# Attention scores in blocks of 57 queries by 64 keys, two to a tile, with the value product in quadrants of the array

## The chip, the core and the metric

The kernel runs on one core of a Trainium2 chip. The metric is the device time in microseconds (us), the median of several runs; smaller is better. The engines are TensorE (PE; its weight loads are PEld), VectorE (DVE), ScalarE (ACT), GpSimd (POOL) and SyncE (SP), the last two used here mostly to issue transfers (DMA). TensorE writes to PSUM, which here is one tensor `PS` of four slots with two banks each.

## What is computed

Everything is bfloat16, S = 2048 rows, D = 640. `x = A_q`, and the result is `g * a + (1 - g) * b` with `g = sigmoid((x * gate_w).sum(-1))`.

- `a` is a long convolution: `k` goes through a four-tap causal filter, is multiplied by `v`, convolved over the whole length with the kernels `ssm_k` (an FFT of length 4096 in the reference), and multiplied by `x`.
- `b` is local attention with 32 heads of 20 channels. A query looks at 8 keys, 2 apart, itself included:

```python
qkv = (x @ wqkv).reshape(B, S, 3, H, Dh)          # H = 32, Dh = 20
idx = pos[:, None] - off[None, :]                 # off = 0, 2, 4, ..., 14; only idx >= 0 counts
logits = einsum("bhsd,bhswd->bhsw", q, kg) * Dh ** -0.5
o = einsum("bhsw,bhswd->bhsd", softmax(logits), vg)
b = o.reshape(B, S, D) @ wo
```

## The kernel before

Even and odd rows are kept apart (`xT`: 1024 rows of each parity), so that the 8 keys of a query become 8 neighbours. Attention then works on blocks: 114 queries against 121 keys (114 + 7), 9 blocks for each parity, 18 in all. Heads go in 8 sets `t` of four; each head of a set has its own 32 partitions in the key tile `kb` and the query tile `qb` (20 rows of data, 11 rows of a mask that makes every pair outside the band very negative). In the order of the data:

- `xpose` (L444) transposes x. `qkproj` (L573) makes q and k, 300 matmuls; its fragments go by DMA into `kb` and `qb` (`fragger`, L623, on POOL's and SP's queues). `vproj` (L526) makes `VW`, the v of one block with its keys on the partitions, and a column of ones behind each head's 20 channels.
- `score_gen` (L647): a group is 3 or 4 blocks by four heads. Each matmul has 31 contracted rows, 128 columns and 114 queries, with the four heads in the four row tiles of the array. Two exponentials (L658) turn a group into `ETall`, 121 x 912 or 121 x 684 elements. In the last two sets, filler matmuls (L652) into unused columns follow each group.
- `pv_gen` (L682): `ETall` is the stationary operand, 121 keys by 128 queries, `VW` the moving one. VectorE takes the reciprocal of the ones' column (L692) and multiplies (L694) into `oS`, which lies in `VW`'s memory.
- The convolution is done by transforms in two halves P = 0, 1: `s1_unit` (L709 for the data `u`, L713 for the kernel `h`), `s2_unit` (L732), `products` on VectorE (L764), `inverse1` (L843) and `final` (L930). `h_lin` holds one half of `ssm_k`; the second half is loaded when the first has been used (L324). `Hw` is a copy of `h` with its halves swapped by DMA (L828). `UC` takes the data's transform; its memory is that of the attention's tiles, so that it starts after the last value product.
- `op_tr` (L861) transposes `oS` into `oT`, one PSUM slot of bfloat16 for each of five `ft`, evicted by one copy of 2048 elements. `outproj` (L877) multiplies by `wo`; the evictions (L891) scale by 1 - g into `bl`, and `final` adds (L941, L943, L950) and stores (L952). The last tile goes another way (L882).
- `gate` (L539) makes g; its result takes four small transfers (L548) to come to its place.
- `copy` (L244 on ScalarE, L246 on VectorE) does most evictions, so its lines stand for many places; the tile names tell them apart.

What runs when is written out by hand in `ORDER`: a string with a letter for each stream (`a` is `xpose`, `d` is `score_gen`, `e` is `pv_gen`, and so on), where a letter lets that stream issue its next step and a `-` ahead of it picks VectorE in place of ScalarE (or the second of two engines). All engines work through their own queues in that order; PSUM slots are given out in it too (`take`, `give`). The costs in `Req` do not matter at run time.

Of the kernel before, what the change touches and what calls it, by code (L numbers as in the profile page):

```python
# [18 lines left out]
D = 640  # L19
# [8 lines left out]
BK = 121  # L28
NBP = 9
# [187 lines left out]
def kernel(  # L217
# [41 lines left out]
    ident = p0.tile([128, 128], BF, name="ident")  # L259
    F = p0.tile([128, 512], BF, name="F")  # L260
# [30 lines left out]
    ETall = pR.tile([128, NET, 2, 3 * BQ + 128], BF, name="ETall")  # L291
# [106 lines left out]
    def heads():  # L398
# [120 lines left out]
    def vproj(hp):  # L519
        for j in range(NBP):  # L520
            for par in range(2):
                g = yield Req("P", 0.0, xdeps(BQ * j - PRE, BQ * j - PRE + BK) + [ev(f"Wv{hp}")], take=1, half=1, pe=(5, 136.0, 272.0, 126.0))
                ps = psum(g)
                s0 = X0 + HP * par + BQ * j - PRE
                for dt in range(NDT):
                    nc.tensor.matmul(ps[0:BK, 0:320], lhsT=xT[:, dt, s0:s0 + BK], rhs=Wv[:, dt, 320 * hp:320 * hp + 320],  # L526
                                     start=(dt == 0), stop=(dt == NDT - 1))
# [465 lines left out]
```

## Time and profile before

| | |
|---|---|
| median of 3 runs | 220.84 us (220.32 to 221.04) |
| the profiled execution | 219.82 us, span 218.0 us, granted clock 0.99 |
| PE busy | 205.2 us (94% of the span), 3642 matmuls |
| DVE busy | 183.4 us (84%) |
| ACT busy | 173.5 us (80%) |
| exponentials (L658) | 63.9 us, 80 of them |
| q and k projection (L573) | 49.8 us, 300 matmuls |
| v projection (L526) | 27.5 us, 180 matmuls |
| value product (L682) | 18.5 us, 576 matmuls |
| scores (L647) | 15.6 us, 576 matmuls |

A group's row gives its line, engine, operation, what it writes and reads with the shapes, its count, then busy time in us and the mean ns of one, and the idle time ahead of it with what ended it. Matmuls overlap, so the mean ns of one says nothing of the pace: that is read from how long a run of them holds the chain. The chain of waits gives start, length and what ran.

### The profile page before, as it was taken

Reading aid. Unit: us, or ns where it says so; the run is one execution under the profiler, and the core shown is the slowest. Engines: PE = TensorE matmul, PEld = TensorE weight load, DVE = VectorE, ACT = ScalarE, POOL = GpSimd, SP = SyncE. Lnnn points to the kernel's source line nnn. Section 1 sums busy time; section 2 is a strip of 40 time slices with the busy share of each in tenths; the row PEclk is TensorE's granted clock in tenths of the full one; section 3 lists DMA queues with packets and bytes.
Section 4 is the critical chain, followed back from the end, with each engine's and each line's share of the span. In section 5 each row is a group of like instructions: output and inputs, shape, how many; then the busy total and the mean of one; then the engine's idle time right before and its main releaser. Section 6 shows DMA issues by size and latency. Waiting matters only on the chain.

```text
span 218.0 us, 8528 instructions
## 1 busy us (share of the span) xinstructions
PE 205.2 (94%) x3642; PEld 166.8 (76%) x3642; DVE 183.4 (84%) x264; ACT 173.5 (80%) x251; POOL 50.8 (23%) x129
## 2 busy tenths in 40 slices
PE   6999999999999999999997988999999999999990
PEld 3876987696677677656685766899888999998880
DVE  6647778997998998789897968998999997898782
ACT  0354387769998998989998988999899999487760
POOL 7980811460517045405420000000000000000000
PEclk9999999999999999999999699999999999999999
DMA  6999799699954993899984196767449064003544
GB/s 199 349 251 287 205 185 188 137 168 154 272 160 102 150 146 64 152 150 151 168 160 107 31 223 140 174 158 226 110 110 289 7 149 95 3 3 96 139 128 131
DMA packets 69049, 33.35 MB, mean 153 GB/s; under 512 B 51476, under 2 KB 66708, under 8 KB 69012
## 3 DMA queue, kind: packets, MB, share of 16 engines
q1 hardware_dynamic: 65684, 27.66, 62.0%
q0 software_dynamic: 2880, 4.90, 9.6%
q8 instruction: 28, 0.46, 1.0%
q10 hardware_dynamic: 448, 0.26, 0.4%
q14 instruction: 9, 0.07, 0.1%
HBM read 19.51 MB, written 2.62 MB: 102 GB/s over the span
## 4 chain that ended last, share of the span: by engine, by line
PE 66%; DVE 12%; ACT 6%; SPq 6%; DMA 5%; issue 3%; DVEq 0%; ACTq 0%
PE PS L573 16%; PE PS L526 12%; PE PS L877 10%; PE PS L843 8%; ACT ETall L658 5%; PE PS L682 5%; SPq L324 5%; PE PS L647 4%; PE PS L732 3%; DVE UC L246 3%; DMA h_lin<-in_A_ssm_k_dram 3%; DVE SX L246 3%; PE PS L930 2%; DMA WvT<-in_B_wqkv_dram 2%; PE PS L444 2%
## 5 line engine op out<-in xcount | busy, mean ns | idle before, releaser
L658 ACT ACTIVATE ETall<-PS 121x912 bf16<-121x912 f32 (+1 forms) x80 | 63.9, 865 | 6.4 <-PE PS L647 6.0
L573 PE MATMUL PS<-xT,Wqk 128*128 128x342 bf16 (+1 forms) x300 | 49.8, 310 | 0.7 <-ACT stg L244 0.3
L244 ACT CAST UC<-PS 128x1024 bf16<-128x1024 f32 (+2 forms) x49 | 44.4, 1030 | 4.0 <-DVE UC L246 3.1
L573 PEld LDWEIGHTS <-Wqk 128*128 128x128 bf16 x300 | 27.3, 97 | 14.6 <-issue 0.5
L526 PE MATMUL PS<-WvT,xT 128*121 128x320 bf16 x180 | 27.5, 301 | 0.6 <-DMA WvT<-in_B_wqkv_dram 0.3
L472 DVE TENSOR_TENSOR KX<-KX 128x1280 bf16<-128x1280 bf16 x32 | 25.3, 820 | 0.3
L526 PEld LDWEIGHTS <-xT 128*121 128x121 bf16 x180 | 23.5, 134 | 2.2 <-issue 0.4
L623 POOL DMA_DIRECT2D qb<-stg x29 | 14.5, 504 | 43.3 <-ACT stg L244 27.1
L877 PE MATMUL PS<-wo,oT 128*128 128x320 bf16 x160 | 24.5, 302 | 0.1
L244 ACT CAST stg<-PS 128x363 bf16<-128x363 f32 (+1 forms) x39 | 17.1, 472 | 8.5 <-PE PS L573 8.2
L877 PEld LDWEIGHTS <-oT 128*128 128x128 bf16 x160 | 21.0, 145 | 1.5 <-issue 0.5
L623 POOL DMA_DIRECT2D kb<-stg x36 | 18.0, 510 | 14.8 <-ACT stg L244 7.6
L732 PEld LDWEIGHTS <-G 64*128 64x128 bf16 x512 | 18.1, 93 | 3.8 <-issue 2.5
L682 PEld LDWEIGHTS <-ETall 121*128 121x128 bf16 x576 | 17.8, 97 | 1.6 <-issue 0.2
L682 PE MATMUL PS<-VW,ETall 121*128 121x63 bf16 (+2 forms) x576 | 18.5, 186 | 0.1
L843 PE MATMUL PS<-F,Hw 128*128 128x128 bf16 x160 | 18.1, 219 | 0.0
L843 PEld LDWEIGHTS <-Hw 128*128 128x128 bf16 x160 | 17.9, 114 | 0.0
L647 PE MATMUL PS<-qb,kb 31*128 31x114 bf16 x576 | 15.6, 212 | 2.3 <-ACT ETall L658 1.2
L246 DVE CAST UC<-PS 128x1024 bf16<-128x1024 f32 x13 | 15.3, 1220 | 2.6 <-ACT UC L244 1.2
L647 PEld LDWEIGHTS <-kb 31*128 31x128 bf16 x576 | 9.3, 93 | 10.3 <-issue 8.8
L246 DVE CAST SX<-PS 128x1024 bf16<-128x1024 f32 (+2 forms) x13 | 14.6, 1159 | 2.8 <-PE PS L732 1.7
L891 ACT ACTIVATE bl<-PS,omg 128x320 bf16<-128x320 f32 x30 | 15.4, 566 | 1.9 <-PE PS L877 1.4
(75 smaller groups left out, 329.9 us busy)
## 6 DMA issues: line engine op xcount, KB each, us to landing
xn<-in_A_q_dram SPq DMA_DIRECT2D x8, 320.0 KB
h_lin<-in_A_ssm_k_dram SPq DMA_DIRECT2D x16, 160.0 KB
vin<-in_A_v_dram SPq DMA_DIRECT2D x8, 320.0 KB
Hw<-H SPq DMA_DIRECT2D x8, 320.0 KB
q<-in_A_q_dram SPq DMA_DIRECT2D x8, 320.0 KB
Hw<-SX SPq DMA_DIRECT2D x8, 320.0 KB
kb<-stg POOLq DMA_DIRECT2D x28, 85.1 KB, 4.1
out_dram<-q SPq DMA_DIRECT2D x16, 120.0 KB
```

The costliest lines, as they stand in the source:

```text
L244: nc.scalar.copy(dst, src)
L246: nc.vector.tensor_copy(dst, src)
L472: eng.tensor_tensor(d, kin[:, n + 3 - j:n + 3 - j + m, :], w.to_broadcast([128, m, QC]), ALU.mult)
L526: nc.tensor.matmul(ps[0:BK, 0:320], lhsT=xT[:, dt, s0:s0 + BK], rhs=Wv[:, dt, 320 * hp:320 * hp + 320], start=(dt == 0), stop=(dt == NDT - 1))
L573: nc.tensor.matmul(ps[:, 0:n], lhsT=Wqk[:, dt, w, 128 * ft:128 * ft + 128], rhs=xT[:, dt, s0:s0 + n], start=(dt == 0), stop=(dt == NDT - 1))
L623: (nc.sync if near else nc.gpsimd).dma_start(dst[r0:r0 + rows, 0:wd], stg[fa - f0:fb - f0, 0:wd])
L647: nc.tensor.matmul(psum(g, h4 // 2)[:, h4 % 2, BQ * bb:BQ * bb + BQ], lhsT=kb[r:r + DH + NF, BK * b:BK * b + 128], rhs=qb[r:r + DH + NF, B ...
L658: nc.scalar.activation(ETall[0:BK, e, :, 0:BQ * nb], psum(g, k)[0:BK, :, 0:BQ * nb], ACT.Exp, scale=SCALE)
L682: nc.tensor.matmul(O[:, (b - b0) // 6, c0:c0 + 21 * nh], lhsT=ETall[0:BK, e, hh, BQ * bb:BQ * bb + 128], rhs=VW[0:BK, b, 4 * t + h4:4 * t ...
L732: nc.tensor.matmul(ps[:, c, 160 * jj:160 * jj + 160], lhsT=G[rows, j0 + jj, 64 - 64 * rr:192 - 64 * rr], rhs=Am[rows, rr].rearrange("p o ( ...
L843: nc.tensor.matmul(d, lhsT=st[(key, P)][:, c, o + il // 4, :, il % 4], rhs=M[:, k, :], start=(k == 0), stop=(k == 1), skip_group_check=True)
L877: nc.tensor.matmul(op, lhsT=oT[:, ft].rearrange("p h m a -> p a (h m)")[:, t, :], rhs=wo[:, ft, 320 * n:320 * n + 320], start=(ft == 0), s ...
```

## The change

All attention uses blocks of half the size. A block of 114 queries is cut in two of 57 queries (`SQ`) with 64 keys (`SK`) each, 57 + 7. The two halves stand one above the other on the 128 partitions of a score tile: a score matmul has 64 columns and 57 queries and goes to partitions 0 to 63 or 64 to 127. `ETall` then has half as many columns to a block; three groups of six blocks take the place of five of three or four, and each exponential has 128 x 684 elements. `vproj` computes the 64 keys of both halves, in two column tiles. In the value product each half has its own 64 x 64 quadrant of the array, keys 0 to 63 to queries 0 to 63 and 64 to 127 to 64 to 127, with rows 57 to 63 of each half unused, and two heads beside each other where it was three. So `oS` has its queries at rows 0 to 56 and 64 to 120, and `op_tr` brings them together by a matmul with a selection matrix `pick` in place of the transposes, in float32, two units for each `ft` with 1024 elements each. There are ten `ETall` buffers in place of nine, fewer fillers, a wait of the two last evictions for the addition to the tile ahead, and a new `ORDER`.

```diff
+SQ = 57
+SK = 64
+NEW = 0
-NET = 9
-GROUPS = [[0, 1, 2, 3], [4, 5, 6, 7], [8, 9, 10, 11], [12, 13, 14], [15, 16, 17]]
-PARTS = [((0, 1, 2), 0, 2), ((3, 4), 12, 1)]
+NET = 10
+GROUPS = [[[0, 1, 2, 3], [4, 5, 6, 7], [8, 9, 10, 11], [12, 13, 14], [15, 16, 17]],
+          [[0, 1, 2, 3, 4, 5], [6, 7, 8, 9, 10, 11], [12, 13, 14, 15, 16, 17]]]
+PARTS = [[((0, 1, 2), 0, 2), ((3, 4), 12, 1)], [((0, 1), 0, 2), ((2,), 12, 1)]]
...
 ORDER = """
...
-i-iiidfifddiiiieiifiiffiieidddiiiiiicddiwdxwexxxxxxxxxxccccffcfffffffffeccc-xcfcccccccccccccccccccccccccccccccccccccccccccidi-ii
+-iicfwcx-iciicicdff-iwcifccdfcifcdccffcccxiicixicxccfccccdcidccccfficcfcdciccicfiiccixccfccccccicecieceie-xi-iiccfccxxdfiiddcc-i
...
@@ vproj
+                split = 4 * hp >= NEW
+                rows = 2 * SK if split else BK
...
+                    for i in range(2 if split else 0):
+                        nc.tensor.matmul(ps[SK * i:SK * i + SK, 0:320], lhsT=xT[:, dt, s0 + SQ * i:s0 + SQ * i + SK], rhs=rhs,
+                                         start=(dt == 0), stop=(dt == NDT - 1), tile_position=(0, SK * i), skip_group_check=True)
@@ score_gen
+                        for i in range(1 + split):
+                            c, q = BK * b + SQ * i, BQ * b + SQ * i
+                            nc.tensor.matmul(psum(g, h4 // 2)[SK * i:SK * i + SK, h4 % 2, bw * bb:bw * bb + bw] if split else ...,
+                                             lhsT=kb[r:r + DH + NF, c:c + (SK if split else 128)], rhs=qb[r:r + DH + NF, q:q + bw],
+                                             start=True, stop=True, tile_position=(r, SK * i), skip_group_check=True)
-                for n in range(0 if t < 6 else (2 if nb == 3 else (14 if t == 6 else 7))):
+                for n in range(0 if t < 6 else (((5 if t == 6 else 3)) if split else ...)):
@@ pv_gen
+                                nh = min(2 if split else 3, 4 - h4)
+                                for i in range(1 + split):
+                                    rows = slice(SK * i, SK * i + SK) if split else slice(0, BK)
+                                    out = slice(SK * i, SK * i + SK) if split else slice(0, 2 * SK)
+                                    q0 = SK * bb if split else 2 * SK * bb
+                                    nc.tensor.matmul(O[out, (b - b0) // 6, cs], lhsT=ETall[rows, e, hh, q0:q0 + (SK if split else 2 * SK)],
+                                                     rhs=VW[rows, b, 4 * t + h4:4 * t + h4 + nh, :].rearrange("p h e -> p (h e)"),
+                                                     start=True, stop=True, tile_position=(SK * i, SK * i), skip_group_check=True)
@@ op_tr
-            tr = psum(g, dt=BF)
-                nc.tensor.transpose(tr[:, par, BQ * j:BQ * j + w], oS[0:w, b, 128 * ft:128 * ft + 128], ident[0:w, 0:w])
-            copy(r.eng, oT[:, ft].rearrange("p h m a -> p m h a"), tr.rearrange("p r (n h a) -> p (r n) h a", h=2, a=16))
+            for par in range(2):
...
+                            nc.tensor.matmul(tr[:, q0:q1], lhsT=oS[0:BK, NBP * par + j, 128 * ft:128 * ft + 128],
+                                             rhs=pick[0:BK, q0 - BQ * j:q1 - BQ * j], start=True, stop=True, skip_group_check=True)
+                copy(r.eng, oT[:, ft].rearrange("p h m a -> p m h a")[:, 32 * par:32 * par + 32], tr.rearrange("p (n h a) -> p n h a", h=2, a=16))
@@ outproj
-                    yield Req("D", 400.0, [g.done, ev(f"z{t}")], give=g.banks)
+                    yield Req("D", 400.0, [g.done, ev(f"z{t}")] + ([ev(f"a{t - 1}")] if n else []), give=g.banks)
```

What `ORDER` does is seen on the queues. On SP's queue, between the loads of v and the copies of `h`, before:

```order
L324 DMA vin<-in_A_v_dram 32x64x80 x8
L548 DMA g_nat<-WvT 32x1x16 x4
L324 DMA h_lin<-in_A_ssm_k_dram 32x40x64 x8
L828 DMA Hw<-H_289 64x5x512 x2
L904 DMA q_2428<-in_A_q_dram 32x8x640
```

and after:

```order
L329 DMA vin<-in_A_v_dram 32x64x80 x8
L329 DMA h_lin<-in_A_ssm_k_dram 32x40x64 x8
L561 DMA g_nat<-WvT 32x1x16 x4
L854 DMA Hw<-H_307 64x5x512 x4
L933 DMA q_3347<-in_A_q_dram 32x8x640
```

The second half of `h_lin` has moved ahead of the gate's four transfers. On VectorE, from the last value product's reciprocal to the first products of the transforms (`SX` is the second half of `h`, `H` the first), before:

```order
L692 RECIPROCAL rd_88<-PS 114x24
L694 TENSOR_TENSOR VW<-PS,rd_88 114x6x80
L246 CAST SX<-PS 128x80x12
L246 CAST SX<-PS 128x80x8
L246 CAST UC<-PS 128x2x512 x8
L246 COPY oT<-PS 128x64x2x16 x3
L764 TENSOR_TENSOR H_289<-UC,H_289 128x80x12
L764 TENSOR_TENSOR Hw<-UC,Hw 128x80x12
```

and after:

```order
L718 RECIPROCAL rd_89<-PS 121x24
L720 TENSOR_TENSOR VW<-PS,rd_89 121x6x80
L250 CAST SX<-PS 128x80x12
L250 CAST UC<-PS 128x2x512
L250 CAST SX<-PS 128x80x12 x2
L250 CAST SX<-PS 128x80x8
L250 CAST UC<-PS 128x2x512 x6
L250 CAST oT<-PS 128x32x2x16
L250 CAST UC<-PS 128x80x12
L790 TENSOR_TENSOR H_307<-UC,H_307 128x80x12
L250 CAST oT<-PS 128x32x2x16
L790 TENSOR_TENSOR Hw<-UC,Hw 128x80x12
```

More evictions now stand between the two, and those of `oT` lie among the products.

More of the change, by code (lines that the diff above doesn't have):

```diff
@@ L290 @@
         ksets.append(kb); qsets.append(qb)
-    ETall = pR.tile([128, NET, 2, 3 * BQ + 128], BF, name="ETall")
+    ETall = pR.tile([128, NET, 2, 6 * SK], BF, name="ETall")
     rds = []
@@ L436, in heads @@
             masks(e)
+        for i in range(2):
+            nc.gpsimd.tensor_copy(pick[:, SQ * i:SQ * i + SQ], ident[:, SK * i:SK * i + SQ])
     def xpose():
@@ L640, in score_gen @@
             kb, qb = ksets[t % 3], qsets[t % 3]
-            for gi, blocks in enumerate(GROUPS):
+            split = t >= NEW
+            bw = SQ if split else BQ
+            for gi, blocks in enumerate(GROUPS[split]):
                 nb = len(blocks)
-                g = yield Req("P", 0.0, [ev(f"set{t}")] + ([ev(f"near{t}")] if t < 2 else []), take=2, pe=(4 * nb, 11.8, 30.0, 11.8))
+                g = yield Req("P", 0.0, [ev(f"set{t}")] + ([ev(f"near{t}")] if t < 2 else []), take=2, pe=(4 * nb * (1 + split), 11.8, 30.0, 11.8))
                 for bb, b in enumerate(blocks):
@@ L654, in score_gen @@
+                w = 512 - bw * nb
+                for n in range(0 if t < 6 else (((5 if t == 6 else 3)) if split else (2 if nb == 3 else (14 if t == 6 else 7)))):
+                    nc.tensor.matmul(psum(g, 1)[:, 1, bw * nb:512], lhsT=mm[:, 0:128], rhs=mm[:, 0:w], start=True, stop=True, skip_group_check=True)
+                if gi == len(GROUPS[split]) - 1:
                     mark(f"sc{t}", g)
+                rows = 2 * SK if split else BK
                 for k in range(2):
                     e = s % NET
-                    r = yield Req("A", 68.0 + 0.834 * 2 * BQ * nb, [g.done, etfree[e], ev("ET")], give=[g.banks[k]])
@@ L658, in score_gen @@
-                    nc.scalar.activation(ETall[0:BK, e, :, 0:BQ * nb], psum(g, k)[0:BK, :, 0:BQ * nb], ACT.Exp, scale=SCALE)
+                    r = yield Req("A", 68.0 + 0.834 * 2 * bw * nb, [g.done, etfree[e], ev("ET")], give=[g.banks[k]])
+                    nc.scalar.activation(ETall[0:rows, e].rearrange("p h (c q) -> p h c q", q=SK)[:, :, 0:bw * nb // SQ, 0:SQ],
+                                         psum(g, k)[0:rows, :, 0:bw * nb].rearrange("p h (c q) -> p h c q", q=SQ), ACT.Exp, scale=SCALE)
@@ L666, in pv_gen @@
         for t in range(NT):
-            for gis, b0, na in PARTS:
-                mm_ = sum(4 * len(GROUPS[gi]) for gi in gis)
-                blocks = [b for gi in gis for b in GROUPS[gi]]
+            split = t >= NEW
+            groups = GROUPS[split]
+            for gis, b0, na in PARTS[split]:
+                mm_ = sum(4 * len(groups[gi]) for gi in gis) * (1 + split)
+                blocks = [b for gi in gis for b in groups[gi]]
                 g = yield Req("P", 0.0, [ev(f"e{t}{gi}{k}") for gi in gis for k in range(2)] + [ev(f"VW{t // 4}{b}") for b in blocks], take=1, half=na % 2,
```

61 lines of the change are left out of this document (29 added, 32 removed).

## The prediction

> **What bounds the kernel now.** I read the page's busy times, then the chain of waits, then the busy time in ten-microsecond stretches, and last the groups of instructions inside the stretch where TensorE is not full.
>
> ```profile
> PE 205.2 (94%) x3642; PEld 166.8 (76%) x3642; DVE 183.4 (84%) x264; ACT 173.5 (80%) x251; POOL 50.8 (23%) x129
> PE 66%; DVE 12%; ACT 6%; SPq 6%; DMA 5%; issue 3%; DVEq 0%; ACTq 0%
> 80.00:90.00 10.00, 10.00 (x182) 7.74 (x181) 9.16 (x15) 8.41 (x14) 5.60 (x20) 1.00 0.47 100
> 120.00:130.00 10.00, 8.93 (x217) 7.18 (x214) 7.95 (x9) 8.83 (x12) 0.19 (x1) 0.83 0.59 121
> 170.00:180.00 10.00, 10.00 (x174) 9.41 (x173) 10.00 (x19) 10.00 (x16) 0.00 (x0) 1.00 0.40 87
> ```
>
> TensorE carries two thirds of the chain. In the stretches (length; busy time of PE, PEld, DVE, ACT, POOL; granted clock; DMA) it is full up to 90 us and again after 140. Only from 90 to 140 us has it holes, while ScalarE is nearly full; the clock there once drops to 0.83. From 140 to 180 us VectorE and ScalarE are full too. So a ScalarE saving can pay only where TensorE waits for it, and VectorE work added after 140 us is not free.
>
> A PE group's busy time hides idle time, because matmuls are pipelined. So I price what TensorE did from 90 to 140 us, with paces from the chain (start, length, what), and the two timeline rows at 74 us:
>
> ```profile
> L682 PE MATMUL PS<-VW,ETall 121*128 121x63 bf16 (+2 forms) x288 | 9.4, 187 | 0.1
> L573 PE MATMUL PS<-xT,Wqk 128*128 128x349 bf16 (+1 forms) x55 | 9.3, 310 | 0.3 <-ACT stg L244 0.3
> L647 PE MATMUL PS<-qb,kb 31*128 31x114 bf16 x272 | 7.8, 212 | 2.3 <-ACT ETall L658 1.2 <-DVE SX L246 0.7 <-DVE H L246 0.2
> L732 PE MATMUL PS<-SX,G 64*128 64x160 bf16 x124 | 5.7, 228 | 0.7 <-ACT ETall L658 0.2
> L732 PE MATMUL PS<-H,G 64*128 64x160 bf16 x128 | 5.4, 228 | 0.5 <-ACT ETall L658 0.4
> L713 PE MATMUL PS<-F,h_lin 64*128 64x128 bf16 x80 | 4.3, 255 | 0.6 <-ACT ETall L658 0.4 <-DVE h_lin L781 0.2
> L652 PE MATMUL PS<-mm 128*128 128x56 bf16 (+1 forms) x71 | 4.0, 194 | 0.0
> ```
> ```profile
> 10.67 1.47 PE PS L573 x10
> 21.23 8.15 PE PS L526 x60
> 45.07 0.65 PE PS L682 x24
> 85.21 0.78 PE PS L713 x24
> 93.98 1.19 PE PS L539 x20
> 119.48 0.47 PE PS L652 x14
> 170.64 0.94 PE PS L732 x24
> 193.66 0.96 PE PS L930 x96
> 200.64 0.69 PE PS L930 x64
> ```
> ```profile
> 74.22 0.81 PE L682 MATMUL PS<-VW,ETall 121*128 121x63 bf16 x24
> 74.96 0.39 PE L647 MATMUL PS<-qb,kb 31*128 31x114 bf16 x16
> 75.28 0.90 PE L573 MATMUL PS<-xT,Wqk 128*128 128x342 bf16 x5
> ```
>
> A value product costs 0.65/24 = 27 ns. The same 24 before a score group take 74.96 − 74.22 = 0.74 us: 0.09 us is what a change of the array's tile shape costs. A score matmul, without that, costs (75.28 − 74.96 − 0.09)/16 = 14 ns. In the same way L732 costs 35 ns (252 in the stretch), L713 29 ns, a filler 27 ns (14 of L652; 74 ns for the eight wide ones, half of L573's 147). The stretch then holds 7.8 (L682) + 8.1 (L573) + 3.8 (L647) + 8.8 (L732) + 2.3 + 2.3 + 2.5 (ten of L526 at 136 ns, and the gate) + 50 changes of shape × 0.09 = 40 us of work in 50: about 9.9 us of slack. Two things made it, both in the chain:
>
> ```profile
> 97.45 0.55 SPq L548
> ...
> 109.81 6.23 DMA h_lin<-in_A_ssm_k_dram
> 117.13 0.60 PE PS L713 x8
> ...
> 132.00 1.71 ACT ETall L658 x2
> ```
>
> The second load of h_lin stands on SP's queue behind the gate's four transfers (L548), which wait for ScalarE; it lands at 116 us. After that TensorE waits for exponentials.
>
> **The change, part by part.**
>
> Exponentials. The score tile of a block shrinks from 121 x 114 to 128 x 57.
>
> ```profile
> L658 ACT ACTIVATE ETall<-PS 121x912 bf16<-121x912 f32 x48 | 41.9, 944 | 2.1 <-PE PS L647 1.9
> L658 ACT ACTIVATE ETall<-PS 121x684 bf16<-121x684 f32 x32 | 22.1, 745 | 4.3 <-PE PS L647 4.1
> ```
>
> It was 80 of them in 41.9 + 22.1 = 64.0 us; it becomes 48 of the 684-column kind, 48 × 22.1/32 = 33.2 us. ScalarE loses 31 us, all ahead of the last value product. It is worth only TensorE's slack. The h_lin load now stands ahead of the gate on SP, so that it no longer waits for ScalarE; the gate's transfers come after it, and their users, the evictions of the output projection, only behind the attention. Of the 9.9 us I take two thirds, **−6.7 us**; the ends are 0 (both engines must still alternate, score to exponential to product) and −9.9.
>
> Scores: 576 matmuls become 1152 in eight tiles of 32 x 64. The nearest rows are those of sixteen tiles, L930: (0.96 − 0.69)/32 = 8.4 ns each. 1152 × 8.4 − 576 × 14 = 9.7 − 8.1 = **+1.6 us**; the ends are 8.1 us in all (a pair costs one old matmul) and 16.1 (no pair overlaps).
>
> Value product: 576 become 1152 in two diagonal quadrants. If a pair runs side by side at the old pace nothing changes, **0**. The lower end is 10 ns each (0.96/96), −4.1 us; the upper is 27 ns each, **+15.6 us**. That shapes in different rows and columns overlap is what L930 shows, so I stand near the lower half. The load of the stationary operand speaks for a little more:
>
> ```profile
> L526 PEld LDWEIGHTS <-xT 128*121 128x121 bf16 x180 | 23.5, 134 | 2.2 <-issue 0.4 <-DVE xT L246 0.4
> L682 PEld LDWEIGHTS <-ETall 121*128 121x128 bf16 x576 | 17.8, 97 | 1.6 <-issue 0.2
> L539 PEld LDWEIGHTS <-wgz 128*32 128x32 bf16 x20 | 0.4, 96 | 0.6 <-issue 0.3
> ```
>
> [...] By (134 − 96)/89 = 0.43 ns per column a load of 64 takes 14 ns more than now. Unhidden that makes a pair 41 ns, +8 us; loads under a running matmul are hidden in most rows, so I leave it in the range. [...]
>
> Projection of v: 180 matmuls of 121 columns become 360 of 64 in two column tiles. L539 is such a case with four: 20 of 512 columns in 1.19 us are 60 ns each, where L526's 136 ns for 320 makes 218 for 512. They overlap, so a pair costs 136 ns as now: **0**. Ends: 0, and 180 × 136 ns = +24.5 us if they did not.
>
> Changes of shape: the order has 130 of them before and 156 after, 18 more ahead of the last value product and 8 behind it: +1.6 and +0.7 us. Score groups fall from 40 to 24, but value and v groups now have shapes of their own.
>
> Two copies of 57 columns join POOL ahead of the first fragments, and the last two evictions of VectorE wait for an addition that already stood ahead of them there: nothing, POOL being 23% busy. Fillers: 63 × 27 + 8 × 74 ns become 24 × 74: **−0.5 us**. Twelve of L732 move behind the last value product: −0.4 and +0.4.
>
> So the part up to the last value product: −6.7 + 1.6 + 1.6 − 0.5 − 0.4 = **−4.4 us**.
>
> After it. The second half of the inverse (L843) needs the last product on VectorE.
>
> ```profile
> 175.20 17.10 PE PS L843 x304
> 181.79 0.51 DVE L764 TENSOR_TENSOR Hw<-UC,Hw 128x640 bf16<-128x640 bf16 x1
> 139.80:179.00 39.20, 38.64 (x582) 35.05 (x577) 38.01 (x54) 38.26 (x50) 0.56 (x3) 1.00 0.59 151
> ```
>
> VectorE ends at 182.3. The second half starts 144 × 56 ns after 175.20, at 183.3: 1.0 us to spare. VectorE had 1.2 us idle in those 39.
>
> ```profile
> L246 DVE CAST UC<-PS 128x1024 bf16<-128x1024 f32 x13 | 15.3, 1220 | 2.6 <-ACT UC L244 1.2 <-PE PS L709 0.7 <-PE PS L843 0.6
> L246 DVE CAST SX<-PS 128x960 bf16<-128x960 f32 x6 | 6.8, 1154 | 1.8 <-PE PS L732 1.7
> L246 DVE COPY oT<-PS 128x2048 bf16<-128x2048 bf16 x5 | 5.9, 1218 | 0.3 <-PE PS L861 0.3
> L908 DVE TENSOR_SCALAR q<-q,g_nat 128x640 bf16<-128x640 bf16 x16 | 4.9, 393 | 0.0
> ```
>
> The transposes of the output become matmuls into f32, so five evictions of 2048 become ten of 1024, no shorter each; eight fall to VectorE: 8 × 1.18 − 5.9 = +3.5 us. The new order also puts there two more SX and two more UC evictions of 960 (+4.5), one UC of 1024 less (−1.2), three output evictions (+1.5, by 0.5 each) and two scalings of q (+0.6): +8.9, of which the idle time takes 1.2. TensorE also comes later by its own work: 25 more matmuls of the output projection stand ahead of that point (3.4 us, taken from the end), the transposes 0.3, L732 0.4, ten changes of shape 0.9, 5.0 in all. VectorE is late by 7.7 − 1.0 − 5.0 = 1.7 us. To the end: 0.7 + 0.4 + 0.3 + 1.7 = **+3.1 us**.
>
> The sum is −4.4 + 3.1 = −1.3 us. Against the profiled execution, 219.82 us (span 218.0), that makes 218.5; that execution lay 1.0 below the median of 220.84, so the median comes to **219.5 us**.
>
> **Rivals.**
> - *The pair of quadrants does not overlap.* Both write one bank of PSUM, on different partitions; in L930, L732 and L647 matmuls of different rows write different banks, so nothing here excludes it. Place: each of 16 value-product groups, on TensorE. +15.6 us: 235. It decides from 27 + 1.3/0.576 = 29 ns a pair. Against it: L539's column tiles share a bank and overlap. [...] No trace here has the case.
> - *VectorE carries the end.* If its added 7.7 us reach the end whole, because the evictions also hold up TensorE, the part behind costs 7.7 + 1.4, not 3.1: 225.5. For it: VectorE and ScalarE are both full from 160 to 180 us.
> - *The slack stays.* TensorE's holes change their cause only: +6.7, 226. Against it: ScalarE loses 31 us.
> - *TensorE gets cheaper.* Product pairs at 20 ns (−4.0), which the lower end allows, and half of the remaining slack (−1.6): 214. For it: sixteen tiles give 8.4 ns a matmul.
>
> **Chances.** The forecast 0.44 (own range 216.5 to 222), quadrants serial 0.10, VectorE 0.17, slack 0.12, cheaper 0.17. About 0.3% (0.7 us) is what can be told from no change. Faster: 0.17 and 0.29 of the forecast's 0.44, 0.46. Same: 0.10 of the forecast and 0.04 of VectorE's, 0.14. Slower: 0.05 + 0.13 + 0.12 + 0.10 = 0.40. The range leaves out the serial case and some of the two tails: 213 to 228.
>
> **What would show it.** Value products in groups of 96 that take 1.3 us are right, 2.6 wrong. v groups at 0.68 us per 10. Exponentials 48 at 0.69 us of busy time each. No DMA of h_lin in the chain. The last value product some 4 us earlier. The last L764 product, and whether the second half of the inverse waits for it. It is wrong if a tile shape costs more than the rows of other shapes say, or if TensorE waits elsewhere before 90 us.

## The result, and the profile after

The changed kernel takes 242.96 us (median of 4, 242.17 to 247.5) where the kernel before, run beside it, takes 220.94 (median of 4, 220.32 to 221.81): 1.098 times as long, with a 95% interval of 1.092 to 1.104. (The ratio leaves out the execution of 247.5 us, which is over 1.5% above the fastest.) 219.5 was predicted, with 228.0 as the upper end of the range. The profiled execution has a span of 241.5 us, against 218.0.

First the page of the changed kernel: busy times, busy share of TensorE and its clock in 40 slices, the queue that carries instructions (packets, MB, share), and the shares of the chain. The last row is that queue in the kernel before.

```profile
PE 216.9 (90%) x4937; PEld 169.2 (70%) x4937; DVE 180.5 (75%) x260; ACT 155.0 (64%) x228; POOL 51.2 (21%) x131
PE   6999999989987899999988957999968999998892
PEclk9999999999999799999999965599999999999998
q8 instruction: 38, 0.62, 1.2%
PE 75%; DVE 7%; ACT 6%; issue 6%; DMA 4%; DVEq 0%; POOL 0%; SPq 0%; ACTq 0%
```
```profile
q8 instruction: 28, 0.46, 1.0%
```

ScalarE lost its work as forecast. But "issue", time in which the engine waits for nothing that the profile shows, has doubled to 6%; the clock has a hole of three slices (and a smaller one ahead of it); and ten more packets of 16 KB came over the queue of instructions. The chain shows where (start, length, what):

```profile
75.05 0.86 PE PS L708 x48
75.90 0.50 PE PS L664 x48
76.40 0.55 PE PS L586 x3
76.95 2.13 issue
79.09 3.42 PE PS L586 x12
...
137.53 1.63 PE PS L708 x96
139.37 2.96 issue
...
145.26 1.62 issue
147.13 0.54 PE PS L669 x3
147.67 2.66 PE PS L708 x49
150.33 1.72 PE PS L758 x24
```

(L664 are scores, L669 fillers, L708 value products, L586 the q and k projection, L758 the second transform step.) TensorE stops with nothing to wait for, in the middle of a group of the q and k projection for 2.1 us and inside two score groups for 3.0 and 1.6 us, and what follows runs slowly: 12 of L586 in 3.42 us, where 15 take 2.29 elsewhere; 49 value products in 2.66, where 48 took 0.86 at 75.05. The stretches (busy time of PE, PEld, DVE, ACT, POOL; clock; DMA) show the same:

```profile
130.00:140.00 10.00, 8.44 (x384) 6.71 (x378) 7.06 (x8) 7.39 (x10) 0.19 (x1) 1.00 0.58 136
140.00:150.00 10.00, 6.05 (x222) 5.24 (x224) 2.32 (x6) 2.89 (x4) 0.37 (x2) 0.54 0.96 236
150.00:160.00 10.00, 10.00 (x154) 8.36 (x150) 5.87 (x7) 5.73 (x7) 0.00 (x1) 0.61 0.35 81
```

From 140 to 150 us no engine is full and the clock is at half. The last value product starts at 153.4 us, where it was 138.5; the part behind it takes 88.0 us in place of 79.5. So 14.9 us are lost ahead of that point and 8.5 behind it.

The gaps have one thing in common. Numbering TensorE's instructions in the order of the trace (a weight load and a matmul are two), all stops of over 0.43 us ahead of an instruction that waits for no semaphore are these (from the start of the last instruction ahead of the stop to the start of the next, so a little longer than the idle time in the chain):

```
at us    gap us   instruction number
 66.44    1.01     2240 =  8*256 + 192
 76.64    2.44     2752 = 10*256 + 192
 98.29    0.63     3776 = 14*256 + 192
102.86    0.71     4032 = 15*256 + 192
124.18    0.88     5312 = 20*256 + 192
139.18    3.15     6336 = 24*256 + 192
145.02    1.86     6592 = 25*256 + 192
226.00    1.30     9408 = 36*256 + 192
```

A packet of 16 KB on that queue stands for 256 instructions: 38 packets for 9918, 28 for 7324 before. The packet that lands ahead of a stop's end began to move only after TensorE had passed the number one piece earlier, 1.2 to 2.8 us after it at these eight stops; where it lands too late, TensorE stands still until 1.3 to 1.7 us behind the landing (140.94 and 142.33 us, 145.54 and 146.88 are two of them). Ahead of the gap at 139.18 TensorE had used 256 instructions in 2.57 us; the two stops at 98.29 and 102.86 follow 256 that took 4.4 and 3.9 us, so there the piece was late rather than the use fast. From one number 256k + 192 to the next the kernel before never takes under 3.2 us, and it has no stop of that length. I call this theory S, the supply of instructions. In the expectations, rival O is the new order, Q the price of quadrants and small tiles, W waits for other engines, and F that a piece has a time of its own, whatever other transfers do.

### The profile page after: what moved, and what is told of

It is laid out like the page before. It is cut to its first block, busy times and chain, and to the rows that moved or that the text cites. A ratio compares the mean times of both kernels' runs of the same rounds, so it can differ in the third digit from the quotient of the medians.

```text
span 241.5 us, 11047 instructions
## 1 busy us (share of the span) xinstructions
PE 216.9 (90%) x4937; PEld 169.2 (70%) x4937; DVE 180.5 (75%) x260; ACT 155.0 (64%) x228; POOL 51.2 (21%) x131
## 4 chain that ended last, share of the span: by engine, by line
PE 75%; DVE 7%; ACT 6%; issue 6%; DMA 4%; DVEq 0%; POOL 0%; SPq 0%; ACTq 0%
PE PS L586 19%; PE PS L539 11%; PE PS L708 8%; PE PS L906 8%; PE PS L758 7%; PE PS L869 7%; PE PS L664 5%; ACT UC L248 4%; DMA kb<-stg 3%; DVE UC L250 2%; PE PS L959 2%; PE PS L739 2%; DVE oT L250 2%; DMA WvT<-in_B_wqkv_dram 2%; PE PS L451 1%
## 5 line engine op out<-in xcount | busy, mean ns | idle before, releaser
L586 PE MATMUL PS<-xT,Wqk 128*128 128x342 bf16 (+1 forms) x300 | 51.8, 317 | 2.2 <-issue 2.1
L676 ACT ACTIVATE ETall<-PS 128x684 bf16<-128x684 f32 x48 | 35.0, 756 | 15.4 <-PE PS L664 12.0
L586 PEld LDWEIGHTS <-Wqk 128*128 128x128 bf16 x300 | 27.0, 99 | 18.7 <-issue 4.6
L539 PE MATMUL PS<-WvT,xT 128*64 128x320 bf16 x360 | 29.6, 309 | 1.4 <-issue 0.7
L539 PEld LDWEIGHTS <-xT 128*64 128x64 bf16 x360 | 19.3, 113 | 9.2 <-issue 4.9
L708 PEld LDWEIGHTS <-ETall 64*64 64x64 bf16 x1152 | 21.7, 117 | 3.7 <-issue 3.0
L708 PE MATMUL PS<-VW,ETall 64*64 64x42 bf16 (+1 forms) x1152 | 23.4, 188 | 0.5 <-issue 0.5
L758 PEld LDWEIGHTS <-G 64*128 64x128 bf16 x512 | 18.9, 97 | 6.0 <-issue 4.3
L664 PE MATMUL PS<-qb,kb 31*64 31x57 bf16 x1152 | 15.0, 202 | 6.8 <-issue 5.3
L664 PEld LDWEIGHTS <-kb 31*64 31x64 bf16 x1152 | 11.5, 107 | 12.9 <-issue 11.0
L718 DVE RECIPROCAL rd<-PS 121x48 f32<-121x48 f32 (+1 forms) x16 | 6.1, 381 | 15.3 <-PE PS L708 14.9
L250 DVE CAST SX<-PS 128x960 bf16<-128x960 f32 (+2 forms) x12 | 13.5, 1149 | 5.1 <-PE PS L758 2.6
L248 ACT CAST H<-PS 128x960 bf16<-128x960 f32 (+2 forms) x16 | 15.1, 971 | 2.4 <-issue 2.2
```

The costliest lines, as they stand in the source:

```text
L248: nc.scalar.copy(dst, src)
L250: nc.vector.tensor_copy(dst, src)
L539: nc.tensor.matmul(ps[SK * i:SK * i + SK, 0:320], lhsT=xT[:, dt, s0 + SQ * i:s0 + SQ * i + SK], rhs=rhs, start=(dt == 0), stop=(dt == NDT ...
L586: nc.tensor.matmul(ps[:, 0:n], lhsT=Wqk[:, dt, w, 128 * ft:128 * ft + 128], rhs=xT[:, dt, s0:s0 + n], start=(dt == 0), stop=(dt == NDT - 1))
L664: nc.tensor.matmul(psum(g, h4 // 2)[SK * i:SK * i + SK, h4 % 2, bw * bb:bw * bb + bw] if split else psum(g, h4 // 2)[:, h4 % 2, bw * bb:bw ...
L676: nc.scalar.activation(ETall[0:rows, e].rearrange("p h (c q) -> p h c q", q=SK)[:, :, 0:bw * nb // SQ, 0:SQ], psum(g, k)[0:rows, :, 0:bw * ...
```

## Experiments

"Gaps" are, as above, stops of over 0.43 us ahead of an instruction without a wait. In all the profiles there were 106 of them behind the first transposes (in `burst` also within its own matmuls), and all 106 stand at 256k + 192. At each of the 106, TensorE goes on 1.2 to 1.9 us after the piece that begins at this number has landed, and that piece began to move 0.2 to 5.5 us after TensorE had passed the number 256 earlier. Where it passes such a number without a pause of over 0.43 us (492 cases), the piece had landed at least 0.9 us ahead; at the stops it had landed at most 1.1 us ahead or not yet. Times of "last PV" (the last value product) and half clock come from each run's one profile; the times of a kernel with gaps scatter by 1 to 3%, and so does what its profile shows (those of order_old, pv_full and late_dma3 are of executions of 248.2, 234.6 and 254.5 us, above the medians).

| run | median us | ratio to before (95%) | TensorE instr. | last PV | behind it | gaps | half clock to last PV |
|---|---|---|---|---|---|---|---|
| before | 220.2 to 220.9 | 1 | 7324 | 138.5 | 79.5 | 0 | 3.4 |
| after | 242.96 | 1.098 (1.092 to 1.104) | 9918 | 153.4 | 88.0 | 8, 12.0 us | 16.0 |
| order_old | 246.03 | 1.112 (1.103 to 1.120) | 9914 | 161.1 | 85.3 | 6, 11.9 us | 24.5 |
| shift32 | 247.03 (one) | | 9982 | 156.4 | 87.7 | 11, 16.1 us | 21.5 |
| before_pad | 237.86 | 1.074 (1.064 to 1.083) | 9628 | 156.6 | 80.2 | 5, 7.9 us | 11.9 |
| before_wide | 225.98 | 1.026 (1.022 to 1.030) | 7772 | 144.0 | 80.2 | 2, 1.2 us | 0 |
| pv_full | 232.26 | 1.049 (1.040 to 1.058) | 8766 | 140.9 | 91.8 | 6, 9.1 us | 6.7 |
| pv_sc_full | 219.48 | 0.992 (0.989 to 0.995) | 7614 | 131.0 | 86.3 | 3, 3.7 us | 0 |
| pv_sc_pad | 243.02 | 1.103 (1.096 to 1.111) | 9918 | 155.0 | 87.8 | 9, 15.7 us | 23.9 |
| pv_sc_exp2 | 235.70 | 1.071 (1.063 to 1.079) | 7614 | 145.9 | 86.9 | 2, 1.8 us | 3.4 |
| before_exp | 222.79 | 1.011 (1.003 to 1.018) | 7324 | 140.8 | 79.1 | 1, 0.5 us | 3.4 |
| before_optr | 229.15 | 1.039 (1.032 to 1.047) | 7344 | 141.1 | 85.9 | 1, 1.0 us | 0 |
| old_tr | 242.80 | 1.101 (1.095 to 1.107) | 9898 | 156.2 | 83.8 | 9, 15.0 us | 18.8 |
| pv_full_tr | 232.75 | 1.048 (1.040 to 1.057) | 8746 | 143.1 | 84.7 | 7, 8.8 us | 9.4 |
| late_dma3 | 250.05 | 1.127 (1.121 to 1.134) | 9919 | 154.9 | 97.7 | 9, 14.1 us | 15.6 |

### Is it the number of instructions, the order or the shapes?

**pv_full**: one value product for a pair of halves.

```diff
-for i in range(1 + split):
-    rows = slice(SK * i, SK * i + SK)
-    ... lhsT=ETall[rows, e, hh, q0:q0 + SK], tile_position=(SK * i, SK * i)
+for i in range(1):
+    rows = slice(0, 2 * SK)
+    ... lhsT=ETall[rows, e, hh, q0:q0 + 2 * SK], tile_position=(0, 0)
```

> The changed kernel (242.96 us), where each pair of 64x64 value products is one product of 128 rows and 128 columns with the same 42 to 63 result columns; it mixes the two halves of a block, and for the last block of a group reads the columns of the block before, so that the attention part of the result is another. It has 576 matmuls, that is 1152 TensorE instructions, less; the time of a value product falls by 4.5 ns a pair (31.5 to 27), 2.6 us in all. Theory S (instruction supply: where small matmuls stand densely, TensorE uses up its instructions faster than the pieces of 256 are fetched, and the slow clock follows from those gaps): the gaps named issue in the chain (about 12 us over the kernel) fall to under 4 us, the clock stays at full speed between 130 and 160 us, and the time comes to 222 to 229 us. Rival O (the new order of the work) and rival W (waits for other engines): 239 to 242 us. Rival Q (the price of quadrants): 2.6 us less, 240.

Measured 232.26: 10.7 less, far more than the product's own price, yet short of what S said. Gaps are fewer but not gone (9.1 us), and the clock falls to half after three of them; the scores are still as dense as before.

**order_old**: the change's attention in the old order.

```diff
-ORDER = <the changed kernel's>
+ORDER = <that of before; per set, the steps of score groups 1 and 3 of 5 left out; each eviction of op_tr doubled>
```

> The changed kernel's attention in the order of work of the kernel before: of five score groups of a tile the second and the fourth are dropped, since three now hold the same blocks, and each eviction of the transposed output is doubled in place. Rival O (the new order costs the time): 218 to 225 us. Theory S: the same 9876 TensorE instructions stand as densely, if in other places; gaps named issue stay, 6 us or more of them, and the time is 230 to 245 us.

246.03: the order isn't to blame, and the old one is no better. The gaps now stand elsewhere in the work, at the same kind of number.

**before_pad**: pads in the kernel before.

```diff
 nc.tensor.matmul(..., lhsT=kb[r:r + 31, BK * b:BK * b + 128], rhs=qb[r:r + 31, BQ * b:BQ * b + BQ], ...)
+for n in range(2):
+    nc.tensor.matmul(psum(g, h4 // 2)[:, h4 % 2, 511 - n:512 - n], lhsT=<the same>, rhs=qb[r:r + 31, BQ * b:BQ * b + 1], ...)
```

> The kernel before (220.9 us) with two one-column matmuls of the same tile shape behind each of its 576 score matmuls, written to unused columns of the score bank: 1152 matmuls or 2304 TensorE instructions more, nearly as many as the change adds (2590); nothing else is touched. The pads' own price is 8 to 14 ns each by the scores' rows, 9 to 16 us of TensorE, of which up to 10 us fit into its holes between 90 and 140 us. Theory S: gaps named issue of 0.5 to 3 us appear in the chain, which the kernel before does not have, at instruction numbers that are 192 above a multiple of 256, and the time is 232 to 245 us. Rivals O, W, Q: no such gaps, 221 to 229 us.

237.86, with the gaps foretold. Here are its clock, its queue of instructions and the largest gap in its chain:

```profile
PEclk9999999999999999999997697979999999999999
q8 instruction: 37, 0.61, 1.1%
140.62 3.78 issue
```

A group of 16 scores takes 0.55 us in place of 0.32 with its 32 pads, 7 ns each; all pads are 8.1 us of work, and the kernel lost 17.

**before_wide**: the control, nearly the same work in few instructions (8 or 2 more fillers a group).

```diff
-for n in range(0 if t < 6 else (2 if nb == 3 else (14 if t == 6 else 7))):
+for n in range((2 if nb == 3 else 8) + (0 if t < 6 else (2 if nb == 3 else (14 if t == 6 else 7)))):
```

> The control to before_pad: the kernel before with as much more TensorE work in the same score groups, but in few instructions: eight fillers of 56 columns behind each group of four blocks and two of 170 behind each of three, 224 matmuls (448 instructions) of 27 and 74 ns, 7.6 us, and some 3 us for 34 more changes of tile shape, against 8.1 us for before_pad's 1152 matmuls. Theory S: no gap named issue over 0.6 us, no slow clock beyond that of the kernel before, 220 to 227 us. Rival (TensorE work in these groups costs, however it is cut): 235 to 240 us, as before_pad's 237.9.

225.98: 5.8 us for some 11 us of work, two gaps of 0.6 us, no half clock. So before_pad's loss isn't TensorE's work.

**shift32**: 64 instructions more at the start.

```diff
+for n in range(32):
+    nc.tensor.matmul(wu[:, 0, 0:64], lhsT=z[:, 0:128], rhs=z[:, 0:64], ...)
```

> The changed kernel with 32 more small matmuls (64 instructions, 0.9 us) at its very beginning, where TensorE waits for the first inputs anyway. Theory S: the gaps move with the count, not with the work: they stay at instruction numbers 192 above a multiple of 256, which now means 32 matmuls earlier in the program; 240 to 246 us. Rivals O, W, Q: the gaps stay ahead of the same instructions of the program; 243 us.

All eleven gaps stay at 256k + 192. That at number 2240 stands between two matmuls of `vproj` in the changed kernel, and inside a group of value products here. The 247.03 is one run only, and above the 240 to 246 that were expected.

**pv_sc_full**: scores too are one matmul of 128 keys a pair.

```diff
-for i in range(1 + split):
-    c, q = BK * b + SQ * i, BQ * b + SQ * i
-    ... psum(...)[SK * i:SK * i + SK, ...], lhsT=kb[r:r + 31, c:c + SK], tile_position=(r, SK * i)
+c, q = BK * b, BQ * b
+... psum(...)[:, ...], lhsT=kb[r:r + 31, c:c + 128], tile_position=(r, 0)
```

> pv_full, with each pair of score matmuls also made one, of 128 keys by 57 queries (the second half of a block then scores the first half's queries): 1152 matmuls or 2304 TensorE instructions less than the changed kernel, some 7600 in all against 7324 before; tiling, exponentials, evictions and order are those of the changed kernel. Theory S: no gap named issue over 0.7 us ahead of the last value product, half clock under 4 us, and the last value product ends at 130 to 138 us (138.5 before, 153.4 in the changed kernel); with the part behind it, 84 to 88 us, the time is 217 to 226 us. Rival (the stretch is held up by something else that pv_full only touched): 228 to 233 us.

**pv_sc_pad**: pv_sc_full with before_pad's pads.

> pv_sc_full (219.5 us) with two one-column matmuls of its own tile shape behind each of its 576 score matmuls, as in before_pad: 2304 instructions more, the changed kernel's count again, without one 64x64 quadrant or 64-column tile in the attention. The pads' own work is 7 ns each by before_pad, 8.1 us. Theory S: gaps named issue and half clock come back, the last value product ends at 148 to 158 us, 234 to 246 us. Rival Q (the quadrants and small tiles were what cost, not the count): the pads' own work alone, 222 to 228 us.

219.48 without the pads and 243.02 with them, the changed kernel's time (to 0.1 us by luck: its executions run from 241.6 to 244.8), without a quadrant or a 64-column tile in its attention. Clock and queue of the two, pv_sc_full first:

```profile
PEclk9999999999999999999999999999999999999999
q8 instruction: 29, 0.48, 1.0%
```
```profile
PEclk9999999999979999999999555599999999999997
q8 instruction: 38, 0.62, 1.2%
```

The pads' own work is 8.1 us, so of the 23.5 us between the two some 15.4 are the supply and the clock that follows it. S stands. O and Q fall as the main cause, and W with them, since the gaps stand ahead of instructions that wait for nothing. Two gaps were still there ahead of the last value product in pv_sc_full, of 1.65 and 0.75 us, more than expected (0.7).

### What a piece costs, and whether other transfers matter

**burst**: 1024 one-column matmuls in 32 x 32 tiles at the start of the kernel before.

```diff
+for n in range(1024):
+    c, k = n % 4, n // 4 % 4
+    nc.tensor.matmul(PS[32 * c:32 * c + 32, k, 1, 0:1], lhsT=z[32 * k:32 * k + 32, 0:32], rhs=z[32 * k:32 * k + 32, 0:1], tile_position=(32 * k, 32 * c), ...)
```

> The kernel before with 1024 matmuls of one column in 32x32 tiles at its very start, ahead of the first transposes: the supply of instructions measured by itself. Theory S: 2048 instructions run until those at hand are used up, then in steps of 256, each step 3.3 to 5 us, 13 to 20 ns an instruction; 24 to 36 us in all, and the kernel is about 20 to 30 us longer than 220.6. Rival: 8.4 ns a matmul as in the rows of sixteen tiles, 9 us, without steps.

255.14 (one run), 35 us longer. Its chain, from the start (each step's two rows are a run of matmuls and a wait; the chain's counts leave some out, by the timeline 128 matmuls run between two waits):

```profile
3.92 1.86 PE PS L405 x218
5.78 5.33 issue
11.10 1.17 PE PS L405 x122
12.27 2.83 issue
...
20.28 5.30 issue
25.58 1.17 PE PS L405 x122
26.75 2.55 issue
29.31 1.17 PE PS L405 x122
30.48 2.28 issue
```

128 matmuls run in 1.17 us (9 ns each) and then wait. From 26.75 us on, when nothing else is moved (27 to 36 us hold two packets, both of instructions), a step is 3.45 to 3.73 us: 13.5 to 14.6 ns an instruction, 27 to 29 ns a matmul. While the inputs are loaded, steps are 4.0 us twice and 6.5 us twice.

**late_dma, late_dma2, late_dma3**: the copies of H into Hw behind the last value product. All three move the letters of `swaps`, `load_q` and `load_wo` in `ORDER` there; the third also has, ahead of the first transfer:

```diff
+nc.gpsimd.tensor_copy(Hw[:, 0, 0, 0, 0:1], oS[:, NB - 1, D - 1:D])
```

> The changed kernel with the eight transfers that copy H into Hw, one load of q and that of wo issued behind the last value product instead of from 137 us on; the work on the engines is the same. Theory S with traffic (a piece of instructions arrives later while other transfers fill the DMA engines): the pieces that were begun 3.1 to 5.2 us late at 137 to 150 us come 1 to 2 us after their turn, the two gaps there shrink from 5.0 us together to under 2.5, the 17 us of half clock go, and the time falls from 243 to 230 to 237 us. Rival F (a piece has a fixed time, whatever else moves): gaps and clock stay, 241 to 245 us. In both the products may wait for Hw a little, up to 1 us.

> In the run late_dma the transfers went at the old time: they wait on their own queue for what they copy, not for their place in the order. Here the first copy of H into Hw also waits for a one-column POOL copy that reads the last normalized value product, so that all eight, the loads of q and wo behind them on the queue, start at about 155 us; Hw is first used at 173 us. Theory S with traffic: the pieces of instructions at 137 to 150 us come 1 to 2 us earlier, the two gaps of 5.0 us shrink to under 2.5, half clock lasts 3 to 7 us in place of 17, and the time falls to 232 to 239 us. Rival F (a piece takes its time, whatever else moves; the run burst had steps of 3.5 to 3.7 us without and 4.0 to 6.5 with other traffic): gaps and clock stay, 240 to 245 us.

> late_dma and late_dma2 left the transfers where they were (129.6 to 153.6 us by the trace), the second because its POOL copy was emitted ahead of the value products. Here the copy is emitted behind the last of them, so that the eight transfers of H into Hw and those of q and wo behind them start at about 155 us. Theory S with traffic: pieces of instructions come 1 to 2 us earlier at 137 to 150 us, the two gaps there shrink from 5.0 to under 2.5 us, half clock from 17 to 3 to 7 us, and the last value product ends 4 to 8 us earlier than in the changed kernel; 234 to 240 us, if Hw isn't late. Rival F (a piece has its fixed time): gaps and clock stay, 241 to 245 us.

The first two (244.20 and 243.88) tell nothing: the transfers still started at 131 and 132 us. The third moved them, and 140 to 150 us then hold no other traffic (DMA share 0.02, after 0.96):

```profile
140.00:150.00 10.00, 6.39 (x323) 5.23 (x320) 4.90 (x9) 4.06 (x6) 0.00 (x0) 0.81 0.02 5
```

Pieces there come every 3.3 to 4.2 us (4.7 to 5.2 with the traffic), yet the gaps from 135 to 148 us still add up to 5.3 us (5.0 in two gaps, and some under 0.4, with the traffic): the work uses up the four pieces there in 1.9 to 3.5 us, faster than they come even alone. The last value product is no earlier. So F is nearer: traffic lengthens a piece, but its own time suffices to starve TensorE. That the total is 7 us worse is my edit: Hw came late, and TensorE stood 10.1 us from 174.0 on.

### The prediction's own steps

**before_exp**: half of the exponentials' columns left out of the kernel before.

```diff
-nc.scalar.activation(ETall[0:BK, e, :, 0:BQ * nb], psum(g, k)[0:BK, :, 0:BQ * nb], ACT.Exp, scale=SCALE)
+w = (228, 171)[nb == 3]
+nc.scalar.activation(ETall[0:BK, e, :, 0:w], psum(g, k)[0:BK, :, 0:w], ACT.Exp, scale=SCALE)
```

> The kernel before with exponentials of only half of each score group's columns (456 and 342 elements in place of 912 and 684; the rest of ETall keeps ones, so that the value products of those blocks are of ones). ScalarE loses 64.0 us less about 80 times 0.41, that is some 30 us, as in the change; nothing else is touched. The prediction's step of the slack: TensorE's holes from 90 to 140 us close by two thirds, 212 to 216 us. Rival (the slack stays, the holes only change their cause): 219 to 222 us.

222.79: nothing gained, though ScalarE's exponentials fell from 63.9 to 37.2 us. The chain of before_exp says why:

```profile
101.58 0.74 DVE KX L485
102.35 0.84 DVE KX L487
...
113.16 5.73 DMA h_lin<-in_A_ssm_k_dram
118.89 1.18 issue
120.17 0.53 DVE h_lin L782
120.74 0.60 PE PS L714 x8
121.44 1.24 DVE SX L246
...
125.14 2.36 DVE SX L246 x2
```

The second half of h_lin lands at 118.9 us (116.0 in the kernel before), behind other work on VectorE and SP, and VectorE's evictions follow: the holes changed their cause. The last value product is 2.3 us later, and the part behind it is as long as before, so the 1% arises there; why h_lin lands later isn't settled. The run tests only half of the step, since the change also moves h_lin's load ahead of the gate's transfers, and here it stays behind them.

**pv_sc_exp2**: the exponentials' old work in the new order.

```diff
-nc.scalar.activation(ETall[...][:, :, 0:nb, 0:SQ], psum(g, k)[...], ACT.Exp, scale=SCALE)
+for nx in (nb - 1, nb):
+    nc.scalar.activation(ETall[...][:, :, 0:nx, 0:SQ], psum(g, k)[...], ACT.Exp, scale=SCALE)
```

> pv_sc_full with each exponential preceded by one over five of its six blocks into the same place: 48 activations of about 0.6 us more, so that ScalarE has the exponential work of the kernel before again, 62 to 64 us in place of 35, and the rest stays. The prediction's step of the slack, in the new order: worth two thirds of 9.9 us, so 224 to 229 us. Rival (the saving on ScalarE was worth nothing, as the run before_exp says for the old order): 219 to 222 us.

235.70, 16.2 us above pv_sc_full: more than the step said, and the reverse of before_exp. Chain shares of this run:

```profile
PE 49%; ACT 20%; issue 10%; DVE 10%; DMA 4%; POOL 3%; DVEq 0%; SPq 0%; ACTq 0%; POOLq 0%
```

ScalarE now holds 20% of the chain, and TensorE waits 13.4 us in all for exponentials, where the list of its waits in pv_sc_full has none. The two largest of these waits (us in total, times, longest):

```profile
PE PS L663 <- ACT ETall L675: 5.5, 9, 1.1
PE PS L586 <- ACT ETall L675: 4.0, 8, 0.7
```

(The 10% of "issue" in this chain are mostly one stretch of 12.3 us on POOL; TensorE's own stops come to 1.8 us.) The new order gives ScalarE other work: 155.0 us busy in the changed kernel, where 173.5 less 28.9 of exponentials would be 144.6. In this order the saving pays, in the old one it does not; that the work moved to ScalarE is the reason is likely but not shown, since the order also moves h_lin's load.

**before_optr**: the new way of turning the output, in the kernel before. **old_tr** and **pv_full_tr**: the old way, in the changed kernel and in pv_full. The first, in `op_tr` (the other two the other way round):

```diff
-nc.tensor.transpose(tr[:, par, BQ * j:BQ * j + w], oS[0:w, b, 128 * ft:128 * ft + 128], ident[0:w, 0:w])
+nc.tensor.matmul(tr[:, q0:q1], lhsT=oS[0:BQ, NBP * par + j, 128 * ft:128 * ft + 128], rhs=ident[0:BQ, q0 - BQ * j:q1 - BQ * j], ...)
```

> The kernel before with the changed kernel's way of turning the attention's output: ten groups of matmuls against the identity into f32 with an eviction of 1024 each, in place of five of transposes with evictions of 2048 in bf16; each stands where the one it replaces stood. By the prediction's rows five more evictions of about 1.2 us, in part on VectorE, which then delays the second half of the inverse: 222 to 225 us. Rival (hidden, since ScalarE takes its share): 220 to 221 us. Rival (VectorE holds up TensorE too): 226 to 229 us.

> The changed kernel with the attention's output turned as in the kernel before: five groups of transposes in bf16 with five evictions of 2048, each at the place of the later of the two that it replaces; the 14 of 128 partitions that the change skips are not skipped, so queries stand in another order in the result. By the run before_optr (+8.9 us) this is worth 5 to 9 us: 234 to 238 us. Rival (the part behind the attention is longer only through the clock and the gaps): 241 to 244 us.

> Both at once: one value product a pair of blocks as in pv_full (halves mixed), and the transposes of old_tr (queries in another order). If the two causes add up, 232.3 less the 5 to 9 us of the transposes: 223 to 227 us, which leaves 3 to 6 us to the remaining gaps. Rival (they share one cause): 230 to 233 us.

The three disagree. In the old order the new way costs 8.9 us, of which 6.4 lie behind the last value product; the other 2.5 lie ahead of it, where the edit changes nothing and h_lin lands 2.3 us later in the profile. In the new order the old way brings nothing that the times can tell (242.80 for 242.96, 232.75 for 232.26); by the profiles the part behind the last value product is 83.8 us in old_tr and 86.2 to 88.0 in the changed kernel and the two that left its transfers alone, so some 2 to 4 us, in part because half clock reaches 1.7 us behind that point in old_tr and 4.5 in the changed kernel; the rest is hidden by gaps that vary by more (that at 66 us was 1.0 us long in the changed kernel, 4.5 in old_tr). From pv_full to pv_full_tr it falls from 91.8 to 84.7, with 7.0 us of half clock behind that point in the first and 0.8 in the second. What turning the output costs in the new order stays open.

## Why the prediction was wrong

**The step that failed** is the one that isn't there. The sum priced TensorE's added matmuls (+1.6 us for the scores, 0 for the value product, 0 for the v projection) by their pace in short groups and took it that they are at hand when their turn comes: the supply of instructions stood at nothing, without a reason. In its place the runs show 12.0 us of stops and some 8.8 us lost to half clock behind them. The diff doubles the matmuls of attention and adds 180 to the v projection, and its fastest rows (8.4 ns) are from groups of at most 96. The last sentence of the prediction named the sign ("if TensorE waits elsewhere before 90 us"), with no price.

The size, by the profile of the changed kernel: the gaps are 12.0 us. Half clock costs some 7.1 us ahead of the last value product and 1.7 behind it (each group of the chain in the slow stretches less its length elsewhere, for example 2.66 less 0.88 for 49 value products, 3.42 less 1.83 for 12 of L586). Together 20.8 of the 23.5 us between the two profiles. Without them the last value product would stand at 153.4 − 10.7 − 7.1 = 135.6, and the part behind it would take 88.0 − 1.3 − 1.7 = 85.0: 220.6 against 218.0, an estimate that assumes no new wait in place of a gap. The forecast for that span was 216.7, so the rest of the sum would have missed by some 3.9 us. pv_sc_full bears it out in part: it stands at 219.48, but with some 9.5 us less of TensorE's own work (a pair of scores at 7.5 ns for 17, a full value product at 25 for a pair's 32). pv_sc_pad gives the second size for the supply and its half clock, some 15.4 us. No run pointed to a version of the whole computation that beats the kernel before, so none was tried.

**Up to the last value product**, −4.4 forecast. By the estimate above −2.9. Its terms:

- Scores +1.6: right. 48 take 0.50 us with the change of shape, 8.5 ns each.
- Value product 0: a pair takes (1.62 − 0.09)/48 = 32 ns, not 27, so +2.9 us. So the price of the rival of serial quadrants (54 ns) is wrong. No run times one quadrant alone, so how far two diagonal quadrants on different partitions of one bank overlap is not shown. The estimate from the weight loads' rows, 14 ns more for a load of 64 columns, was right for the load: 110 ns in the median in the changed kernel (`ETall`, L708), 96 for one of 128 columns in the kernel before (L682); the pair took 5 ns more.
- v projection 0: right, 120 in 8.27 us is 138 ns a pair.
- Exponentials: 48 at 35.0 us (0.73 each), forecast 33.2 (0.69).
- Slack −6.7: the mechanism was incomplete. In the old order the same saving gains nothing (before_exp); in the new one, giving it back costs 16.2 us. What pays is the saving together with the new order, which moves h_lin's load ahead of the gate and 10.4 us of other work to ScalarE, which I hadn't counted; no run separates the two, and the step's own size can't be read off either run.

```profile
22.64 8.27 PE PS L539 x120
41.83 0.50 PE PS L664 x48
64.59 1.62 PE PS L708 x96
L676 ACT ACTIVATE ETall<-PS 128x684 bf16<-128x684 f32 x48 | 35.0, 756 | 15.4 <-PE PS L664 12.0 <-PE PS L669 1.7 <-issue 1.1
```

**Behind it**, +3.1 forecast, 5.5 with gap and half clock taken off. The stretch from the last value product to the end of the inverse, in pv_sc_full (full clock) and in the kernel before:

```profile
131.00:193.00 62.00, 58.10 (x894) 53.44 (x891) 59.49 (x90) 53.16 (x67) 0.75 (x4) 1.00 0.53 123
```
```profile
138.50:192.30 53.80, 53.24 (x856) 49.62 (x853) 50.60 (x76) 49.54 (x62) 0.56 (x3) 1.00 0.52 129
```

TensorE's own work there grew by 4.9 us, forecast 5.0. VectorE's work grew by 8.9, forecast 8.9 of which 1.2 in idle time. TensorE's idle time grew from 0.6 to 3.9 us, where VectorE was to be late by 1.7: TensorE waits for the evictions of oT themselves, and not for the last product at the end of VectorE's queue. From 182.05 us to the end of the inverse at 217.13 the chain of the changed kernel holds TensorE alone. That is the mechanism of the rival "VectorE carries the end", at a smaller size. Behind the inverse the 25 output matmuls that moved ahead were to save 3.4 us; 24.4 us in place of 25.7 are 1.3. There the last stage waits for two evictions of UC on ScalarE, which the prediction didn't name, and for a piece of instructions. In the changed kernel these are:

```profile
176.90 2.31 DVE oT L250 x3
179.22 1.00 issue
...
217.17 0.90 ACT UC L248
218.07 1.04 ACT UC L248
...
226.23 1.07 issue
```

Of the list of what would show it, no h_lin transfer stands in the chain of the changed kernel, as said, and the v groups are right to 0.12 us (0.80 with the change of shape for 0.68). The last value product was to come 4 us earlier and came 15 later. No rival described the outcome: the nearest in time, the serial quadrants at 235, has another cause.

## What to carry to other kernels

A matmul is two instructions in these traces (4937 weight loads and 4937 matmuls in the changed kernel), and TensorE here got 256 of them in some 3.5 us without other traffic and 4 to 6.5 with it (run burst; from number to number it was 3.0 to 8.2 us at the 106 stops). 128 matmuls in 3.5 us are 27 ns each; work that ran faster could run dry, however well it overlapped: 128 in 1.17 us in burst, 2.57 us ahead of the stop at 139.18 us in the changed kernel. Before cutting matmuls into smaller tiles, count instructions and the time in which 256 are used at the densest place; after it, look for "issue" in the chain, for the packets on the instruction queue and for half clock behind them. "Issue" alone is not the sign, as pv_sc_exp2 shows: the stop must be TensorE's own. A saving on an engine off the critical path is worth what the order makes of it: test it alone, in both orders.

## What the hardware showed that was not expected

- TensorE's instructions came while the kernel ran, in pieces of 16 KB (28 packets within the span of the kernel before, 38 in the changed kernel), and at the stops each began to move only after TensorE had begun the piece ahead of it (0.2 to 5.5 us after). All 106 stops stand 64 instructions ahead of a multiple of 256; no run shows why they stand there.
- Half clock followed some gaps of 1.4 us and more, in stretches of 3.41 us or a multiple of it: 3.4 us for the 1.4 us at 106.2 in order_old, 17.1 us (five times 3.41) from 140.8 on for the gaps of 3.15 and 1.86 in the changed kernel. It did not always: 1.65 us in pv_sc_full brought none, and the kernel before has 3.4 us of half clock at 121.5 without such a stop.
- At half clock the small value products lose more than half their pace: one of 18 ns (48 in 0.86 us) took 54 (49 in 2.66 us), three times as long. A matmul of L758 took 72 ns for 39 (24 in 1.72 us, 0.94 elsewhere), under twice.
